# Attention and routed experts in one kernel: an attention pipeline one block deeper, and expert 0's rescaling moved between engines

## The chip, the cores and the metric

The kernel runs on one core of one Trainium2 chip. A core has a matrix engine (TensorE, in the profile PE, with its weight loads shown as PEld), VectorE (DVE), ScalarE (ACT), GpSimd (POOL) and SyncE (SP), each with its own queue of instructions that it works through in order, and 16 DMA engines that they share. The metric is device time in microseconds (us) for one execution. Matrix results land in PSUM, from where DVE or ACT copies them on; all other data lies in SBUF.

## What is computed

Eight batches of causal attention with a window of 128 and a slope per head (8 heads, 576 tokens, head size 64) give x, 4608 tokens of 512 values. Then a gate gives each token a weight for each of eight experts, balanced by eight rounds of row and column normalisation, and every expert is applied to every token:

```python
rel = pos[:, None] - pos[None, :]
mask = (rel >= 0) & (rel < 128)
scores = where(mask, scale * q @ k.T - slopes * abs(rel), -1e9)
x = softmax(scores) @ v                  # [4608, 512] after the heads are joined

P = exp(x @ w_gate - max)                # [4608, 8]
for _ in range(8):
    P /= P.sum(1, keepdims=True) + 1e-09
    P /= P.sum(0, keepdims=True) + 1e-09
    P *= N / E
for e in range(8):                       # D = 512, F = 1024
    out += P[:, e:e + 1] * (relu(x @ w1[e]) @ w2[e])
```

## The kernel before

The order of all instructions is written out by hand, so the place of a call in the Python text is its place in its engine's queue.

**Attention (lines 132 to 423).** The 576 tokens of a batch are five blocks of 128 (the last has 64); 40 blocks in all, loop index `i`, batch `b`, block `kb`. For a block, `scores(b, kb, half)` (line 209) multiplies keys and queries for four heads into the PSUM tile psS (one tile of two banks, used by both halves in turn), ACT takes the exponential (line 224) and DVE multiplies by the mask (line 230). `attend` (line 238), called through `finish(i - 1)` for the block before, multiplies by V into psN0 and psN1, one bank for each group of four heads, and DVE divides each group by its row sum (lines 268 and 269) into xsb. `put_x` (line 295), called through `finish2(i - 1)`, transposes xsb on PE into psXT and DVE copies it to xT, the array x of the experts. `gates` (line 279) multiplies xT by the gate's weights.

The queries and keys of the next batch are prepared meanwhile: `load_qk` (line 143, on POOL's queue, three buffers for four loads per batch), `turn` (line 169, two DVE copies, one for k and one for q, each into a buffer of its own), `tr_unit` (line 180, PE transposes; k is copied to KT by ACT, q to QZ by two DVE copies). Block kb of a batch does `tr_unit` for j = kb - 1, for k and for q.

Between these, PE is filled with work of expert 0: a group is 512 tokens, `l1(ft)` is one unit (four matmuls of 512 columns, relu on ACT), `l2(ms)` is two units (eight matmuls, copied to acc by DVE in line 322). `fill(most)` (line 333) takes units from the list while `credit` lasts; a block earns RATE = 2.75. Groups 0 to 5 are done this way, 96 units. psT, psXT, psG, psh and psy share the four buffers of tag pmm. `finish2` adds a group to the list once its tokens are in xT.

**Expert 0's rest and the balancing (lines 450 to 501).** DVE and POOL do the eight rounds on P_sb, while PE runs groups 6 to 8 of expert 0 (`e0_l1`, `e0_l2`, copies on ACT). The last round writes Pe_sb. Then PE transposes P (line 492), DVE copies it (line 497), SP stores it to PTd, and `load_p` (line 511) loads the factors of a step back, broadcast over partitions, as Pb.

**Experts 1 to 7 (lines 503 to 699).** 63 steps, expert `e`, group `g`. `make_xs` multiplies xT by Pb, two DVE operations per step. In a step PE alternates seven products of layer 2 of this step (`product`, eight matmuls of 256 columns each, by a scheme that needs seven products of quarters where eight would be plain; `make_s` and `make_t` prepare its sums) with eight pieces of layer 1 of the next step (`l1s`). The products go to four banks m0 to m3; `gather` (line 604, DVE) adds a bank to a quarter of acc. Before the first gather on a group, acc must hold expert 0's result times its factor, with the quarter (1, 1) subtracted from two others: `convert(g)` (line 609) does this on POOL, four multiplies (line 615) and two subtracts (line 618) per group, all nine groups being queued ahead of step 0. `quad(g, rh, ch)` names a quarter, two blocks of 256 columns.

Of the kernel before, what the change touches and what calls it, by code (L numbers as in the profile page):

```python
# [14 lines left out]
def kernel(  # L15
# [32 lines left out]
    RATE = 2.75  # L48
# [83 lines left out]
    with (  # L132
# [36 lines left out]
        def turn(b: int, half: int):  # L169
            for nm in ("k", "q"):  # L170
                tt = asb.tile(
                    [RP, RT, 4 * Dh], FP16, name=f"{nm}p_{b}_{half}", tag=f"{nm}p", bufs=1
                )
                nc.vector.tensor_copy(
                    out=tt.rearrange("p r (h d) -> p r h d", d=Dh),
                    in_=raw.pop((nm, b, half)).rearrange("p h (r d) -> p r h d", d=Dh),
                )
                turned[nm] = tt
# [30 lines left out]
        def scores(b: int, kb: int, half: int):  # L209
            k0 = kb * P  # L210
# [4 lines left out]
            for jj in range(2):  # L215
# [14 lines left out]
            nc.vector.tensor_tensor(  # L230
                out=pt[0:nk, :, 0:nq],
                in0=pt[0:nk, :, 0:nq],
                in1=maskT[0:nk, 4 * half : 4 * half + 4, 0:nq],
                op=ALU.mult,
            )
            return pt

        def attend(b: int, kb: int, pts, prev):
# [3 lines left out]
            xsb = asb.tile([P, H, Dh], FP16, name=f"xsb_{b}_{kb}", tag="xsb", bufs=2)  # L242
            for hg in range(2):
                psN = aps.tile([P, 4, Dh + 1], FP32, name=f"psN{hg}_{b}_{kb}", tag=f"psN{hg}")
# [14 lines left out]
                for i, (hh, lhsT, rhs) in enumerate(ops):  # L259
                    nc.tensor.matmul(  # L260
                        out=psN[0:nk, hh, :],
                        lhsT=lhsT,
                        rhs=rhs,
                        start=(i == 0),
                        stop=(i == len(ops) - 1),
                    )
                rden = asb.tile([P, 4], FP32, name=f"rden_{b}_{kb}_{hg}", tag="rden", bufs=2)
                nc.vector.reciprocal(out=rden[0:nk, :], in_=psN[0:nk, :, Dh])
                nc.vector.tensor_tensor(
                    out=xsb[0:nk, 4 * hg : 4 * hg + 4, :],  # L270
                    in0=psN[0:nk, :, 0:Dh],
                    in1=rden[0:nk, :].unsqueeze(2).to_broadcast([nk, 4, Dh]),
                    op=ALU.mult,
                )
# [39 lines left out]
        def add_group(g: int):  # L314
# [5 lines left out]
            def l2(ms):  # L320
                psy = l2_mm(0, g, ms, hT0[g], aps, "pmm", 4)
                nc.vector.tensor_copy(out=acc(4 * g + ms), in_=psy)  # L322
# [18 lines left out]
        with tc.manual_schedule():  # L341
# [20 lines left out]
            turn(0, 0)  # L362
# [17 lines left out]

            for i, (b, kb) in enumerate(blocks):
# [4 lines left out]
                a0 = scores(b, kb, 0)  # L386
                if i == 0:
                    turn(0, 1)
# [43 lines left out]
    with (  # L432
# [46 lines left out]
        def e0_l2(g):  # L479
            for ms in range(4):  # L480
                psy = l2_mm(0, g, ms, hT0[g], mps, f"m{ms}", 1)
                nc.scalar.copy(out=acc(4 * g + ms), in_=psy)
# [17 lines left out]
        )  # L500
        e0_l2(NG - 1)

# [106 lines left out]
        def convert(g):  # L609

            for ms in range(2):
                for rh in range(2):
                    p = Pe_sb[:, 0, 4 * g + 2 * rh + ms : 4 * g + 2 * rh + ms + 1]
# [116 lines left out]
```

## Time and profile before

| what | us |
|---|---|
| median of 3 runs | 1129.45 (1129.07 to 1130.6) |
| the profiled execution | 1128.04 |
| its span, first to last instruction | 1126.3 |
| start of block 6 of attention | 51.03 |
| first piece of group 6 of expert 0 | 238.62 |
| transposes of P | 276.08 |
| first product of expert 1 | 291.67 |

A row of the timeline reads: start, duration, engine, line, operation, what it writes and reads, shapes, count, and in brackets the idle time before it and what ended that. Matmuls are pipelined and a row's duration includes the time until the last result is out, so the price of one is read from start to start. L322 is line 322.

### The profile page before, as it was taken

How to read it: one execution, taken by the hardware profiler on the slowest of the kernel's cores; microseconds unless marked ns; L12 is line 12 of the kernel's file. 1: busy time of each engine (PE TensorE's matmuls, PEld its weight loads, DVE VectorE, ACT ScalarE, POOL GpSimd, SP SyncE). 2: the span in 40 equal slices, each digit the busy share in tenths (PEclk: the TensorE clock that was granted, in tenths of full speed). 3: DMA queues.
4: the chain of work that ended last, by engine and by line, in shares of the span. 5: the costliest groups of instructions: out<-in, count | busy, mean ns of one | idle time of the engine just before them, and what ended most of it. 6: DMA issues, size and time to landing. Idle time of an engine off the chain costs nothing.

```text
span 1126.3 us, 18273 instructions
## 1 busy us (share of the span) xinstructions
PE 1061.8 (94%) x7675; PEld 672.0 (60%) x7675; DVE 819.3 (73%) x1320; ACT 439.2 (39%) x737; POOL 166.2 (15%) x155
## 2 busy tenths in 40 slices
PE   3898899899699999999999999999999999999996
PEld 2454455444366666666666666666666666666664
DVE  5777777664498886777676877677777777788885
ACT  3455556534233333333333333333333333333331
POOL 5332222001499700000000000000000000000000
PEclk9999999989899999999999999999999999999999
DMA  9976758122301041003300230014000500003333
GB/s 156 107 73 67 69 62 79 32 40 51 77 20 29 20 75 39 19 20 65 57 19 20 57 57 29 20 26 88 19 20 28 94 20 19 20 10 94 98 97 97
DMA packets 78451, 58.86 MB, mean 52 GB/s; under 512 B 43648, under 2 KB 61472, under 8 KB 78368
## 3 DMA queue, kind: packets, MB, share of 16 engines
q0 software_dynamic: 63376, 30.96, 22.2%
q1 hardware_dynamic: 14992, 26.73, 7.7%
q8 instruction: 60, 0.98, 0.4%
q14 instruction: 23, 0.19, 0.1%
HBM read 79.02 MB, written 9.58 MB: 79 GB/s over the span
## 4 chain that ended last, share of the span: by engine, by line
PE 86%; DVE 6%; ACT 3%; DMA 2%; POOL 1%; issue 1%; DVEq 0%; POOLq 0%; SPq 0%
DMA qf_0_107<-in_q_dram 1%; POOL acc_lo L615 1%; DMA kf_0_82<-in_k_dram 1%; POOL vsb_77 L162 0%; DMA Pb_0_3693<-PTd 0%; DVE acc_hi L607 0%; PE psy_11_1903 L120 0%; POOL acc_lo L618 0%; DVE acc_lo L322 0%; DVE xs_0_3699 L524 0%; DVE xT L309 0%; DMA PTd<-PT_sb 0%; PE M_7_4_11391 L595 0%; PE M_7_5_11530 L595 0%; PE M_7_2_11113 L595 0%
## 5 line engine op out<-in xcount | busy, mean ns | idle before, releaser
L106 PEld LDWEIGHTS <-w1t_103 128*128 128x128 f16 x288 | 27.4, 101 | 32.5 <-issue 6.9
L615 POOL TENSOR_SCALAR acc_lo<-acc_lo,Pe_sb 128x512 f32<-128x512 f32 x24 | 42.1, 1768 | 12.3 <-issue 12.3
L537 PEld LDWEIGHTS <-w1t_2990 128*128 128x128 f16 x288 | 28.4, 98 | 23.9 <-issue 2.2
L537 PEld LDWEIGHTS <-w1t_4981 128*128 128x128 f16 x288 | 28.2, 98 | 20.5
L537 PEld LDWEIGHTS <-w1t_9661 128*128 128x128 f16 x288 | 28.2, 98 | 20.5
L537 PEld LDWEIGHTS <-w1t_6151 128*128 128x128 f16 x288 | 28.2, 98 | 20.5
L537 PEld LDWEIGHTS <-w1t_3689 128*128 128x128 f16 x288 | 28.2, 98 | 20.5
L537 PEld LDWEIGHTS <-w1t_8491 128*128 128x128 f16 x288 | 28.2, 98 | 20.5
L537 PEld LDWEIGHTS <-w1t_7321 128*128 128x128 f16 x288 | 28.2, 98 | 20.5
L615 POOL TENSOR_SCALAR acc_hi<-acc_hi,Pe_sb 128x512 f32<-128x512 f32 x12 | 21.7, 1820 | 0.0
L618 POOL TENSOR_TENSOR acc_lo<-acc_lo 128x512 f32<-128x512 f32 x12 | 17.9, 1514 | 0.5
L162 POOL DMA_DIRECT2D vsb_77<-in_v_dram x20 | 17.1, 877 | 0.3 <-PE psS_1_1_589 L216 0.3
L216 PEld LDWEIGHTS <-KT_73 128*128 128x128 f16 (+1 forms) x80 | 7.5, 111 | 16.1 <-issue 13.4
L162 POOL DMA_DIRECT2D vsb_78<-in_v_dram x20 | 16.9, 874 | 0.0
L95 POOL DMA_DIRECT2D w1t_9661<-in_moe_w_dram x1 | 0.8, 754 | 105.5 <-DVE T_9527 L573 105.5
L95 POOL DMA_DIRECT2D w1t_8491<-in_moe_w_dram x1 | 0.8, 752 | 105.0 <-PE psh_8_7_8351 L537 105.0
L95 POOL DMA_DIRECT2D w1t_7321<-in_moe_w_dram x1 | 0.8, 752 | 105.0 <-PE psh_8_7_7181 L537 105.0
L95 POOL DMA_DIRECT2D w1t_6151<-in_moe_w_dram x1 | 0.8, 752 | 105.0 <-PE psh_8_7_6011 L537 105.0
L285 PEld LDWEIGHTS <-xT 128*128 128x128 f16 x144 | 8.2, 99 | 8.3 <-DVE xT L309 1.5
L216 PEld LDWEIGHTS <-KT_74 128*128 128x128 f16 (+1 forms) x80 | 6.6, 101 | 9.0 <-issue 5.5
L595 PE MATMUL M_1_0_3819<-w2t_3358,hT_0_3759 128*128 128x256 f16 x16 | 2.9, 342 | 7.8 <-DVE acc_lo L607 7.8
L607 DVE TENSOR_TENSOR acc_lo<-acc_lo,M_1_0_3819 128x512 f32<-128x512 f32 x2 | 1.4, 680 | 11.9 <-POOL acc_lo L618 11.9
(3629 smaller groups left out, 3076.9 us busy)
## 6 DMA issues: line engine op xcount, KB each, us to landing
out_dram<-acc_lo SPq DMA_DIRECT2D x48, 128.0 KB
out_dram<-acc_hi SPq DMA_DIRECT2D x24, 128.0 KB
vsb_77<-in_v_dram POOLq DMA_DIRECT2D x16, 128.0 KB, 5.1
vsb_78<-in_v_dram POOLq DMA_DIRECT2D x16, 128.0 KB, 5.2
w1t_103<-in_moe_w_dram POOLq DMA_DIRECT2D x1, 1024.0 KB, 8.2
w2t_113<-in_moe_w_dram POOLq DMA_DIRECT2D x1, 1024.0 KB, 12.3
w1t_2990<-in_moe_w_dram POOLq DMA_DIRECT2D x1, 1024.0 KB, 10.5
w2t_3358<-in_moe_w_dram POOLq DMA_DIRECT2D x1, 1024.0 KB, 9.7
```

Of the source, the lines that this page charges most:

```text
L95: nc.gpsimd.dma_start(out=w1ts[e], in_=w1v)
L106: nc.tensor.matmul(out=psh, lhsT=w1t[:, dt, P * ft : P * ft + P], rhs=xT[:, dt, GT * g : GT * g + GT], start=(dt == 0), stop=(dt == NDT - 1),)
L162: nc.gpsimd.dma_start(out=vsb[0:nk, kb, :, 0:Dh], in_=v[b, :, k0 : k0 + nk, :].rearrange("h s d -> s h d"),)
L216: nc.tensor.matmul(out=ps[0:nk, jj, :, 0:nq], lhsT=KT[:, 2 * half + jj, k0 : k0 + nk], rhs=QZ[:, 2 * half + jj, :, k0 : k0 + nq],)
L285: nc.tensor.matmul(out=psG, lhsT=xT[:, dt, P * blk : P * blk + P], rhs=wg_sb[:, dt, :], start=(dt == 0), stop=(dt == NDT - 1),)
L537: nc.tensor.matmul(out=psh, lhsT=w1ts[e][:, dt, P * ft : P * ft + P], rhs=xss[i][:, dt, :], start=(dt == 0), stop=(dt == NDT - 1),)
L595: nc.tensor.matmul(out=ps[:, ms, :], lhsT=a[:, kt, P * ms : P * ms + P], rhs=b[:, kt, :], start=(first and ms == 0 and kt == 0), stop=(kt ...
L607: nc.vector.tensor_tensor(out=t, in0=t, in1=banks[bank], op=op)
L615: nc.gpsimd.tensor_scalar(out=y, in0=y, scalar1=p, scalar2=None, op0=ALU.mult)
L618: nc.gpsimd.tensor_tensor(out=t, in0=t, in1=quad(g, 1, 1), op=ALU.subtract)
```

## The change

- Attention: `put_x` and the gates of a block come two blocks after its scores, where it was one, and stand between the two halves of scores, as does the first transpose unit; xsb gets a third buffer. The mask is a function of its own: mask0 comes after the first fill and the copy of k, mask1 after `attend`. `turn` takes k or q; k is copied ahead of mask0, q at the end of the block (in block 0 both at the end).
- Division: psN0 and psN1 become one tile of two banks, with one reciprocal and one multiply for all eight heads.
- The copy of expert 0's layer 2 in attention goes from DVE to ACT. RATE is 2.85.
- P's transposes come after two of the four layer 2 pieces of group 7, with the DVE copy and the store.
- `convert` goes. `rescale` does its multiplies on ACT, `rebase` its subtracts on DVE: group 0 before layer 2 of group 8, groups 1 to 8 one in each of the first eight steps. The calls of load_w1(2) and load_w2(2) stand in another place of the text, after the same instructions of their queue.

```diff
-    RATE = 2.75
+    RATE = 2.85
...
-        def turn(b: int, half: int):
-            for nm in ("k", "q"):
+        def turn(b: int, half: int, nm: str):
...
             nc.scalar.activation(
...
-            nc.vector.tensor_tensor(
-                out=pt[0:nk, :, 0:nq],
...
-            return pt
+            def mask():
+                nc.vector.tensor_tensor(
+                    out=pt[0:nk, :, 0:nq],
...
+            return pt, mask
...
-            xsb = asb.tile([P, H, Dh], FP16, name=f"xsb_{b}_{kb}", tag="xsb", bufs=2)
+            xsb = asb.tile([P, H, Dh], FP16, name=f"xsb_{b}_{kb}", tag="xsb", bufs=3)
+            psN = aps.tile([P, 2, GT], FP32, name=f"psN_{b}_{kb}", tag="psN")
+            psV = psN[:, :, 0 : 4 * Dh + 4].rearrange("p g (h d) -> p g h d", d=Dh + 1)
             for hg in range(2):
-                psN = aps.tile([P, 4, Dh + 1], FP32, name=f"psN{hg}_{b}_{kb}", tag=f"psN{hg}")
...
-                        out=psN[0:nk, hh, :],
+                        out=psV[0:nk, hg, hh, :],
...
-                rden = asb.tile([P, 4], FP32, name=f"rden_{b}_{kb}_{hg}", tag="rden", bufs=2)
-                nc.vector.reciprocal(out=rden[0:nk, :], in_=psN[0:nk, :, Dh])
-                nc.vector.tensor_tensor(
-                    out=xsb[0:nk, 4 * hg : 4 * hg + 4, :],
...
+            rden = asb.tile([P, 2, 4], FP32, name=f"rden_{b}_{kb}", tag="rden", bufs=2)
+            nc.vector.reciprocal(out=rden[0:nk], in_=psV[0:nk, :, :, Dh])
+            nc.vector.tensor_tensor(
+                out=xsb[0:nk].rearrange("p (g h) d -> p g h d", g=2),
+                in0=psV[0:nk, :, :, 0:Dh],
+                in1=rden[0:nk].unsqueeze(3).to_broadcast([nk, 2, 4, Dh]),
+                op=ALU.mult,
+            )
...
                 psy = l2_mm(0, g, ms, hT0[g], aps, "pmm", 4)
-                nc.vector.tensor_copy(out=acc(4 * g + ms), in_=psy)
+                nc.scalar.copy(out=acc(4 * g + ms), in_=psy)
...
-                a0 = scores(b, kb, 0)
+                pt0, mask0 = scores(b, kb, 0)
                 if i == 0:
-                    turn(0, 1)
+                    turn(0, 1, "k")
+                    turn(0, 1, "q")
                     for j in range(2, 4):
                         tr_unit(0, "k", j)
                         tr_unit(0, "q", j)
-                fill(1)
-                a1 = scores(b, kb, 1)
-                pts[i] = (a0, a1)
+                if i > 2:
+                    gates(done)
                 if i > 1:
-                    gates(done)
+                    done = finish2(i - 2, xsbs.pop(i - 2))
                 if units:
                     tr_unit(*units[0])
+                fill(1)
+                turning = kb in (0, 2) and b + 1 < B
+                if turning and i > 0:
+                    turn(b + 1, kb // 2, "k")
+                mask0()
+                pt1, mask1 = scores(b, kb, 1)
+                pts[i] = (pt0, pt1)
                 if i > 0:
-                    xsb = finish(i - 1)
+                    xsbs[i - 1] = finish(i - 1)
+                mask1()
                 fill(2)
                 if units:
                     tr_unit(*units[1])
-                if i > 0:
-                    done = finish2(i - 1, xsb)
                 fill(1)
-                if kb in (0, 2) and b + 1 < B:
-                    turn(b + 1, kb // 2)
+                if turning:
+                    if i == 0:
+                        turn(1, 0, "k")
+                    turn(b + 1, kb // 2, "q")
...
             credit = 1e9
-            fill(1)
+            xsbs[i] = finish(i)
             gates(done)
-            xsb = finish(i)
+            done = finish2(i - 1, xsbs[i - 1])
             fill(2)
-            done = finish2(i, xsb)
+            gates(done)
+            done = finish2(i, xsbs[i])
             fill(1 << 20)
             gates(done)
...
-        def e0_l2(g):
-            for ms in range(4):
+        def e0_l2(g, mss=range(4)):
+            for ms in mss:
...
+        def rescale(g):
+
+            for blk in range(4 * g, 4 * g + 4):
+                nc.scalar.mul(acc(blk), acc(blk), Pe_sb[:, 0, blk : blk + 1])
+
+        def rebase(g):
+
+            for rh in range(2):
+                t = quad(g, rh, 1 - rh)
+                nc.vector.tensor_tensor(out=t, in0=t, in1=quad(g, 1, 1), op=ALU.subtract)
+
         g0 = NHI // 4
         e0_l1(g0)
         for g in range(g0 + 1, NG):
             e0_l1(g)
-            e0_l2(g - 1)
+            if g < NG - 1:
+                e0_l2(g - 1)
+        e0_l2(NG - 2, range(2))
         psP = mps.tile([P, 3, P], FP32, name="psP", tag="psP")
...
+        e0_l2(NG - 2, range(2, 4))
+        rescale(0)
+        rebase(0)
         e0_l2(NG - 1)
+        load_w1(2)
+        load_w2(2, per, "w2a")
...
-        load_w1(2)
-        load_w2(2, per, "w2a")
         for i in range(3):
             load_p(i)
         make_xs(0)
         make_xs(1)
-        for g in range(NG):
-            convert(g)
...
             gather(i, 3, 1, 1, ALU.add)
+            if i + 1 < NG:
+                rescale(i + 1)
             if i + 2 < NS:
                 make_xs(i + 2)
+            if i + 1 < NG:
+                rebase(i + 1)
```

More of the change, by code (lines that the diff above doesn't have):

```diff
@@ L167 @@
         turned: dict = {}
-        def turn(b: int, half: int):
-            for nm in ("k", "q"):
[L171 to L178, printed above, removed]
+        def turn(b: int, half: int, nm: str):
+            tt = asb.tile(
+                [RP, RT, 4 * Dh], FP16, name=f"{nm}p_{b}_{half}", tag=f"{nm}p", bufs=1
+            )
+            nc.vector.tensor_copy(
+                out=tt.rearrange("p r (h d) -> p r h d", d=Dh),
+                in_=raw.pop((nm, b, half)).rearrange("p h (r d) -> p r h d", d=Dh),
+            )
+            turned[nm] = tt
         def tr_unit(b: int, nm: str, j: int):
@@ L361 @@
             groups = 0
-            turn(0, 0)
+            turn(0, 0, "k")
+            turn(0, 0, "q")
             for j in range(2):
@@ L379, in finish2 @@
                 return done
+            xsbs: dict = {}
+            done = 0
             for i, (b, kb) in enumerate(blocks):
@@ L607, in gather @@
             nc.vector.tensor_tensor(out=t, in0=t, in1=banks[bank], op=op)
[L609 to L613, printed above, removed]
-                    y = acc(4 * g + 2 * rh + ms)
-                    nc.gpsimd.tensor_scalar(out=y, in0=y, scalar1=p, scalar2=None, op0=ALU.mult)
-            for rh in range(2):
-                t = quad(g, rh, 1 - rh)
-                nc.gpsimd.tensor_tensor(out=t, in0=t, in1=quad(g, 1, 1), op=ALU.subtract)
         def settle(g, rh, ch):
```

13 lines of the change are left out of this document (5 added, 8 removed).

## The prediction

> **What bounds the kernel now.** I read the busy lines first, then the windows by stage (columns: length, then busy us and count of PE, PEld, DVE, ACT, POOL, then granted clock, DMA share, GB/s).
>
> ```profile
> PE 1061.8 (94%) x7675; PEld 672.0 (60%) x7675; DVE 819.3 (73%) x1320; ACT 439.2 (39%) x737; POOL 166.2 (15%) x155
> 28.00:45.00 17.00, 12.59 (x135) 8.49 (x136) 12.31 (x35) 6.33 (x12) 5.71 (x8) 1.00 1.48 152
> 51.03:238.62 187.59, 165.42 (x1669) 92.32 (x1668) 138.46 (x340) 98.34 (x169) 42.15 (x53) 0.97 0.59 62
> 238.62:283.50 44.88, 44.86 (x199) 19.85 (x200) 22.46 (x50) 20.95 (x36) 4.15 (x9) 0.93 0.30 58
> 283.50:311.00 27.50, 18.61 (x103) 10.49 (x103) 13.45 (x18) 8.35 (x14) 14.78 (x11) 0.88 0.32 58
> 600.00:700.00 100.00, 100.00 (x678) 66.25 (x677) 73.64 (x104) 36.84 (x62) 1.64 (x2) 1.00 0.20 40
> ```
>
> PE is the engine that sets the time. From 311 us on it has no gap at full clock, so nothing there can be gained without fewer matmuls, and the change removes none. What can move lies before: attention (to 238.62, where group 6 of expert 0 begins) and the passage to expert 1 (283 to 311). The list of waits says who holds PE there (total, times, longest), and the timeline shows the passage:
>
> ```profile
> PE M_1_0_3819 L595 <- DVE acc_lo L607: 7.8, 1, 7.8
> ...
> PE psXT_1_3165 L300 <- DVE xsb_1_3140 L269: 2.0, 2, 1.8
> ```
>
> Rows of this second kind, one for nearly every block, are the main thing in attention: put_x transposes xsb in the same block in which DVE divides it, and DVE reaches that division only after both masks.
>
> **Part 1: the block pipeline.** A block whose waits are small gives the prices on PE, start to start:
>
> ```profile
> 56.41 0.59 PE L216 MATMUL psS_2_0_651<-QZ_76,KT_74 128*128 128x512 f16 x2
> 56.84 1.03 PE L106 MATMUL psh_0_5_657<-xT,w1t_103 128*128 128x512 f16 x4
> 58.11 0.59 PE L216 MATMUL psS_2_1_663<-QZ_76,KT_74 128*128 128x512 f16 x2 [0.25 <-ACT pt_2_0_654 L224]
> 58.54 0.24 PE L285 MATMUL psG_669<-wg_sb,xT 128*128 128x8 f16 x4
> 58.65 0.42 PE L185 MATMUL psT_k_1_675<-ident,kp_0_568 72*128 72x72 f16 x8
> 58.90 0.29 PE L260 MATMUL psN_1_1_686<-vsb_78,pt_0_0_509 128*128 128x65 f16 x4
> ...
> 59.41 1.02 PE L106 MATMUL psh_0_6_710<-xT,w1t_103 128*128 128x512 f16 x4
> 60.28 1.03 PE L106 MATMUL psh_0_7_716<-xT,w1t_103 128*128 128x512 f16 x4
> 61.14 0.42 PE L185 MATMUL psT_q_1_722<-ident,qp_0_570 72*128 72x72 f16 x8
> 61.40 0.53 PE L300 MATMUL psXT_1_733<-ident,xsb_1_685 128*128 128x128 f16 x4
> 61.77 0.49 PE L216 MATMUL psS_3_0_743<-QZ_76,KT_74 128*128 128x384 f16 x2
> ```
>
> A half of scores is 0.43 (56.41 to 56.84), a unit of filler 0.87 (59.41 to 60.28), a gate 0.11, a set of q or k transposes 0.25, attention times V 0.51 (58.90 to 59.41), put_x 0.37. Without filler a full block is 0.86 + 0.11 + 0.50 + 0.51 + 0.37 = 2.35; blocks 3 and 4 of a batch have narrower scores, block 0 no transposes, so I take 2.1 as the mean (1.9 to 2.35). From 51.03 (block 6) to 238.62 PE has 34 blocks x 2.1 = 71, less 2 for the last batch's absent transposes, plus 94 units x 0.87 = 82 (six groups of 16, two units done), plus 1 for the last block's remainder: 152 us of work in 187.6. **So 36 us are stalls**, and DVE (138 of 188 busy) and ACT (98) are not full.
>
> After the change, in a block at t=0: scores 0.43, gates 0.11, put_x of the block two back 0.37, a transpose 0.25, a unit 0.87, then the second half of scores at 2.0. In the row at 58.11 that half started 1.70 after the first, released by the exponentials; 2.0 is later, so this wait (0.25 where it shows) goes. put_x's division was done a block earlier, so the psXT waits go. DVE loses two small operations per block and the copies of layer 2; ACT gains the copies:
>
> ```profile
> 160.69 0.69 DVE L322 COPY acc_lo<-psy_12_2221 128x512 f32<-128x512 f32 x1
> ...
> 271.10 0.59 ACT L482 COPY acc_hi<-psy_28_3603 128x512 f32<-128x512 f32 x1 [1.13 <-PE psy_28_3603 L120]
> ...
> 224.09 0.17 DVE L268 RECIPROCAL rden_1_0_3150<-psN_7_1_3141 128x4 f32<-128x4 f32 x1
> 224.30 0.42 DVE L269 TENSOR_TENSOR xsb_1_3140<-psN_7_1_3141,rden_1_0_3150 128x256 f16<-128x256 f32 x1
> 224.65 0.17 DVE L268 RECIPROCAL rden_1_1_3162<-psN_7_1_3153 128x4 f32<-128x4 f32 x1
> 224.78 0.28 PE L300 MATMUL psXT_1_3165<-ident,xsb_1_3140 128*128 128x128 f16 x2 [1.78 <-DVE xsb_1_3140 L269]
> ```
>
> 24 x 0.69 = 17 us leave DVE and 24 x 0.59 = 14 come to ACT (98 + 14 = 112 in what would be about 170: covered on average). The pair of divisions is 2 x 0.55 (224.09 to 224.65); as one, a recip of 0.2 and a multiply of 512 elements between 0.42 and 0.84, taken as 0.69 from L322: 0.2 us less per block. Regrouping makes the multiply wait for both head groups; behind it on DVE stand mask1 and the q copies, whose reader is a block away. turn for k now stands ahead of mask0 and splits from q: its data were loaded a batch earlier, its release lets POOL's fourth q/k load and the V loads behind it start a little sooner, and DVE delays mask0 by one copy, whose reader is again a block away.
>
> What is late next? Three things. (a) Where the first fill takes a two-unit piece and the second is empty (about 8 of the 34 blocks by the credit rule), the next scores come 0.43 + 0.51 + 0.25 = 1.2 after the last ones, and 1.7 to 1.9 are needed: 8 x 0.6 = 5. (b) The first fill needs the pmm buffer of the previous block's last q transpose, which DVE frees with two copies of the size of L269's 0.42 behind mask1, some 1.3 after that block's end; PE asks at 1.1: 0.2 in 27 blocks, 5. (c) ACT runs in order with a copy, a k copy, a gate and two exponentials per block: 0.15 x 34 = 5. The end keeps its own chain (mask, division, transpose, copy, gate): 4. That is 19 left of 36, **17 gained** (bounds: 5 if the new waits double, 27 if only the end's and (a) remain). RATE 2.85 for 2.75 only offsets that filler starts a block later: 96 units are consumed either way.
>
> The start: before 45 us PE idles 4.4 of 17 in the window quoted, on the same two kinds of waits, and the first batch's transposes wait behind mask0:
>
> ```profile
> 16.26 0.66 PE L185 MATMUL psT_k_2_176<-ident,kp_1_172 72*128 72x72 f16 x8 [2.45 <-DVE kp_1_172 L174]
> ...
> 31.69 1.01 PE L216 MATMUL psS_2_1_290<-QZ_75,KT_73 128*128 128x512 f16 x2 [1.11 <-ACT pt_2_0_287 L224]
> ```
>
> With turn(0, 1) ahead of mask0 some 1.5 return there, and of the 4.4 most. A new wait: turn(1, 0, "q") and turn(1, 1, "q") hold DVE until their loads land, and the second half of block 1's scores now stands behind a transpose that waits too. I take **5** (0 to 7).
>
> **The clock.** Three short stretches of attention ran at half clock (the first and the last are shown, with what stood before the first), though no wait there is over 1.8:
>
> ```profile
> 72.00:76.00 4.00, 3.62 (x32) 2.02 (x30) 2.58 (x5) 2.12 (x3) 0.00 (x0) 1.00 0.00 0
> ...
> 76.30:79.70 3.40, 2.44 (x9) 0.98 (x10) 2.55 (x8) 0.93 (x1) 0.71 (x2) 0.65 0.00 0
> ...
> 202.60:206.00 3.40, 2.66 (x10) 0.86 (x10) 2.42 (x7) 0.38 (x1) 0.00 (x0) 0.65 0.01 1
> ```
>
> Each costs half of 3.4, together 5, and is in the 36. I count them as returned, as denser work should not trip them. The Trainium skill (TensorE: Matmul & The Clock Gate, Part 1) says that the clock falls after at least one idle window of about 3.4 us. This trace does not agree: the stretch before the first fall was 3.62 of 4.00 busy. By that rule the falls would have another cause than these waits and would stay, which is a rival below.
>
> **Part 2: the passage to expert 1.**
>
> ```profile
> 276.08 0.49 PE L492 MATMUL psP<-identf,Pe_sb 128*96 128x128 f32 x3
> ...
> 282.79 2.36 DVE L524 TENSOR_TENSOR xs_0_3699<-xT,Pb_0_3693 128x1024 f16<-128x1024 f16 x2 [5.62 <-DMA Pb_0_3693<-PTd]
> ...
> 284.06 0.59 PE L537 MATMUL psh_0_0_3760<-xs_0_3699,w1t_2990 128*128 128x512 f16 x2 [0.58 <-DVE xs_0_3699 L524]
> ...
> 285.20 0.59 PE L537 MATMUL psh_0_0_3760<-xs_0_3699,w1t_2990 128*128 128x512 f16 x2 [0.54 <-DVE xs_0_3699 L524]
> ...
> 306.57 1.86 PE L595 MATMUL M_1_0_3819<-w2t_3358,hT_0_3759 128*128 128x256 f16 x8 [7.79 <-DVE acc_lo L607]
> ...
> 308.23 1.61 PE L537 MATMUL psh_1_4_3899<-xs_1_3702,w1t_2990 128*128 128x512 f16 x4
> ...
> 309.68 1.04 PE L595 MATMUL M_1_0_3856<-T_3808,hT_0_3759 128*128 128x256 f16 x8
> ```
>
> and the groups of POOL's convert on the page (busy, mean ns of one, idle before):
>
> ```profile
> L615 POOL TENSOR_SCALAR acc_lo<-acc_lo,Pe_sb 128x512 f32<-128x512 f32 x24 | 42.1, 1768 | 12.3 <-issue 12.3
> ...
> L618 POOL TENSOR_TENSOR acc_lo<-acc_lo 128x512 f32<-128x512 f32 x12 | 17.9, 1514 | 0.5
> ```
>
> PE stops 7.79 at 306.57 because the first gather waits for POOL's convert; two pieces then run at half clock: 306.57 to 308.23 is 1.66 for 0.87 and on to 309.68 is 1.45 for 0.87, 1.4 lost. ACT rescales group 0 during expert 0, so all **9.2** go. P's transposes move ahead of two pieces of layer 2 (2 x 1.73), with their DVE copy, the PTd store and, behind it on SP, the Pb loads. From 276.08 the factors took 6.7 to land; PE now has 3.5 + 6.9 = 10.4 of work over that. New on the way: rescale(0) on ACT follows the copies of group 7 (4.6 after the transposes), 4 x 0.6, then rebase(0) on DVE, 2 x 0.69, ahead of make_xs(0): 8.3, then two halves of 1.18, done at 10.7; the second half is asked for at 11.1. The 0.58 + 0.54 go: **1.1**, with 0.4 us to spare. The weight loads for expert 2 keep their place in POOL's queue.
>
> In expert 1, each of eight steps (13.0 us, fifteen sets of 0.87) gets 4 ACT multiplies and 2 DVE subtracts. ACT is free at 7.8 into the step; the subtracts wait for it, and behind them on DVE stands gather(0, 0, 0), which must end before the next step's first product overwrites bank 0 at 13.0. Free time: 13.0 - 7.8 - 0.7 = 4.5 for 4a + 2d. The trace has no such multiply on ACT: a lies between 0.59 (L482) and 1.77 (L615), d between 0.69 (L322, a DVE operation of that size) and 1.51 (L618). I take the low ends, the rows of the same engines: 3.7, hidden. At the high ends it is 10.1, 5.6 over, 45 us in eight steps. The Trainium skill (ScalarE: Activation LUTs, What ACT_TABLE_LOAD costs) gives 186 ns plus 0.833 ns an element and 93 ns for a per-partition operand; by it, an estimate, a is 0.71 and the sum does not change, though its rules for authors send such multiplies to VectorE.
>
> **The sum.** 17 + 5 + 9.2 + 1.1 = 32.3 us off the profiled execution of 1128.04 (span 1126.3): 1095.7. The median of the runs shown is 1.4 higher: **1097**. Bounds of the terms alone: 5 + 0 + 8 (the stop alone) + 0 = 13 gives 1116, 27 + 7 + 9.2 + 1.1 = 44 gives 1085.
>
> **Rivals.**
>
> - ACT becomes what attention waits for: the layer 2 copies sit in order ahead of exponentials. For: a full block has two exponentials of 1.02 (row below) and four copies of 0.59, 4.4 of the 4.8 that PE needs with its share of filler. Against: 112 of 170 on average. New waits 28 instead of 19, start 3: 1108. Chance 0.22.
> ```profile
> 214.91 1.02 ACT L224 ACTIVATE pt_1_0_3062<-psS_1_0_3059 128x1024 f16<-128x1024 f32 x1 [0.20 <-PE psS_1_0_3059 L216]
> ```
>
> - The clock falls stay, as the page has it: 5 less gained, 1102. Chance 0.10.
> - Attention moves its waits and gains nothing; only the passage pays: 1119. Chance 0.06. That the pipeline does not do what it says is this case.
> - The new waits stay at 9: 1087. Chance 0.06.
> - Slower: the rescaling chain ACT to DVE costs in the steps of expert 1 what it cost on POOL. -32 + 45 gives 1142. It decides from 4a + 2d above 4.5 + 32/8 = 8.5 per step. Against it stand the rows of L482 and L322. Chance 0.03.
>
> The forecast, 1089 to 1104, has 0.53. With the neighbours the range that holds 8 in 10 is **1084 to 1112**; it leaves out the third and the last case and the edges of others. A measurement of this kernel can tell about 0.2% (2.3 us) from no change. Faster 0.96, same 0.01, slower 0.03.
>
> **What would show it.** No psXT wait on xsb and no half clock between 50 and 200 us; group 6 of expert 0 starting near 217 instead of 238.6; no wait of M_1_0 at L607 and no xs wait after the P transposes; steps of expert 1 still 13.0; ACT multiplies near 0.6. It is wrong if PE waits on the pmm buffers or exponentials for over 0.5 us a block, or if DVE's gather comes after 13.0.

## The result: 1094.4 us, and the profile after

| | before | after |
|---|---|---|
| median, us | 1129.29 (4 runs) | 1094.4 (1092.01 to 1095.43, 4 runs) |
| the profiled execution | 1128.04 | 1093.95 |
| its span | 1126.3 | 1092.2 |

The ratio after to before is 0.9686, with an interval of [0.9668, 0.9704]. The kernel is 3.1% faster. Forecast were 1097 us and a range of 1084 to 1112.

First the busy line of the page of after, and its windows by stage (columns as before: length, busy us and count of PE, PEld, DVE, ACT, POOL, then granted clock, DMA share, GB/s):

```profile
PE 1051.2 (96%) x7675; PEld 671.6 (61%) x7675; DVE 795.8 (73%) x1234; ACT 471.1 (43%) x797; POOL 77.2 (7%) x101
```
```profile
37.80:51.40 13.60, 11.93 (x104) 7.28 (x104) 9.88 (x22) 6.00 (x12) 5.35 (x7) 0.54 1.46 141
51.40:211.80 160.40, 153.93 (x1633) 89.96 (x1630) 113.52 (x238) 108.35 (x190) 39.80 (x48) 1.00 0.66 67
211.80:218.60 6.80, 5.50 (x36) 2.53 (x35) 4.46 (x11) 1.56 (x5) 0.39 (x1) 0.58 1.02 148
280.70:293.70 13.00, 13.00 (x90) 8.59 (x89) 10.46 (x15) 7.05 (x12) 0.00 (x0) 1.00 0.08 20
600.00:700.00 100.00, 100.00 (x676) 65.91 (x674) 74.39 (x106) 36.53 (x62) 1.64 (x2) 1.00 0.21 43
```

The number of matmuls is the same, 7675. From block 6 to group 6 of expert 0 PE was 88% busy before (165.42 of 187.59); now it is 96% from 51.4 to 211.8 (153.93 of 160.40), and its clock is full there but for the first 1.1 us. Two half-clock stretches stand on either side, 38.8 to 52.5 and 212.9 to 219.7. The second was there before as well (a granted clock of 0.58 from 236.7 to 243.5); what the first means is said under "The start" below. A step of expert 1 is 13.0 us, without a gap, with the rescaling inside it. From there on nothing has changed.

The timeline of after has the landmarks. Its columns are start, duration, engine, line, operation, output and inputs:

```profile
46.32 1.03 PE L216 MATMUL psS_1_0_532<-QZ_76,KT_74 128*128 128x512 f16 x2
...
214.56 1.87 PE L106 MATMUL psh_6_0_3257<-xT,w1t_103 128*128 128x512 f16 x4
...
248.17 0.49 PE L520 MATMUL psP<-identf,Pe_sb 128*96 128x128 f32 x3
...
259.65 0.59 PE L570 MATMUL psh_0_0_3552<-xs_0_3545,w1t_2842 128*128 128x512 f16 x2 [0.20 <-DVE xs_0_3545 L557]
...
266.13 1.04 PE L628 MATMUL M_1_0_3611<-w2t_3198,hT_0_3551 128*128 128x256 f16 x8
...
273.07 1.04 PE L628 MATMUL M_1_0_3611<-w2t_3198,hT_0_3551 128*128 128x256 f16 x8
```

Read against the landmarks of before, they say where the 34.1 us of span went:

- Block 6 starts at 46.32 instead of 51.03, but two units of filler (2 x 0.87) have moved behind it. The start gave 4.7 - 1.7 = **3.0**.
- From block 6 to group 6 of expert 0: 168.2 us instead of 187.6, with those two units more in it: 19.4 + 1.7 = **21.1**.
- From group 6 to P's transposes 33.6 instead of 37.5, of which 3.5 are the two pieces that moved behind them: 0.4.
- From P's transposes to the first product of expert 1: 17.96, less those 3.5, is 14.5. Before it was 291.67 - 276.08 = 15.6: **1.1**.
- From there to the row at 273.07, the product that waited 7.79 us at 306.57: 6.94 instead of 14.90, **8.0**, and 1.4 for the half clock behind it.
- Step 8 of expert 1 lost 0.6: M_1_8_4733 waits for a sum of `make_s` on DVE.

Together 34.3, against the 34.1 that the spans show.

### The profile page after: what moved, and what is told of

Read it like the earlier page. It is cut to its first block, busy times and chain, and to the rows that moved or that the text cites. A ratio compares the mean times of both kernels' runs of the same rounds, so it can differ in the third digit from the quotient of the medians.

```text
span 1092.2 us, 18188 instructions
## 1 busy us (share of the span) xinstructions
PE 1051.2 (96%) x7675; PEld 671.6 (61%) x7675; DVE 795.8 (73%) x1234; ACT 471.1 (43%) x797; POOL 77.2 (7%) x101
## 4 chain that ended last, share of the span: by engine, by line
PE 91%; DMA 3%; DVE 2%; ACT 1%; POOL 1%; issue 1%; DVEq 0%; ACTq 0%; POOLq 0%
DMA kf_0_404<-in_k_dram 1%; DMA kf_0_105<-in_k_dram 1%; DMA kf_0_82<-in_k_dram 1%; DVE acc_hi L640 0%; POOL vsb_77 L162 0%; POOL vsb_78 L162 0%; DMA Pb_0_3539<-PTd 0%; ACT acc_hi L502 0%; DVE xs_0_3545 L557 0%; PE M_1_8_4733 L628 0%; PE psy_17_2624 L120 0%; PE psy_11_1828 L120 0%; PE psy_18_2704 L120 0%; PE psy_15_2303 L120 0%; PE M_7_7_11644 L628 0%
## 5 line engine op out<-in xcount | busy, mean ns | idle before, releaser
L162 POOL DMA_DIRECT2D vsb_77<-in_v_dram x20 | 18.6, 943 | 0.3 <-PE psG_537 L289 0.3
L162 POOL DMA_DIRECT2D vsb_78<-in_v_dram x20 | 18.2, 926 | 0.0
L508 DVE TENSOR_TENSOR acc_lo<-acc_lo 128x512 f32<-128x512 f32 x12 | 7.8, 688 | 10.9 <-ACT acc_lo L502 10.9
L502 ACT ACTIVATE acc_lo<-acc_lo,Pe_sb 128x512 f32<-128x512 f32 x24 | 15.3, 710 | 0.0
L644 DVE TENSOR_TENSOR acc_lo<-acc_lo 128x512 f32<-128x512 f32 x12 | 8.3, 692 | 0.4
```

Source lines behind the costliest of these rows:

```text
L162: nc.gpsimd.dma_start(out=vsb[0:nk, kb, :, 0:Dh], in_=v[b, :, k0 : k0 + nk, :].rearrange("h s d -> s h d"),)
L502: nc.scalar.mul(acc(blk), acc(blk), Pe_sb[:, 0, blk : blk + 1])
L508: nc.vector.tensor_tensor(out=t, in0=t, in1=quad(g, 1, 1), op=ALU.subtract)
L644: nc.vector.tensor_tensor(out=t, in0=t, in1=quad(g, 1, 1), op=ALU.add)
```

## The experiments

Each time is a median, each ratio that kernel to the kernel before (1129.91 to 1130.81 us in those sessions), with its interval.

**Do the two parts add?** In the first kernel only attention is changed, with the passage (convert on POOL, P's transposes late) as before; in the second only the passage is changed.

> The attention of the changed kernel with the passage to expert 1 of the kernel before (convert on POOL, P's transposes after all of group 7). Theory: the two parts add. Attention took 24 us of the 34 (group 6 of expert 0 began at 214.6 instead of 238.6), so 1129.3 - 24 = 1105 (1102 to 1108), the stop of 7.8 before M_1_0 is there again, and the first piece of group 6 begins at 214.6 as in the changed kernel. Rival: attention only moves its gain into the passage, because the balancing rounds start earlier beside the same PE work; then a part of the 24 is lost again ahead of P's transposes and the time is above 1108.

> The attention of the kernel before with the passage of the changed kernel (rescale on ACT, rebase on DVE, P's transposes two pieces earlier). Theory: 10 us of the 34 are here (7.8 of stop, 1.4 of half clock, 1.4 around the transposes, less 0.6 for a late sum in step 8), 1129.3 - 10 = 1119.5 (1117.5 to 1121); attention keeps its waits of psXT on xsb and its three stretches at half clock. Rival: the passage gains more where attention is slower, or nothing without it: 1115 or 1128.

Measured: attention alone **1103.52** (0.9762 [0.9726, 0.9799]), the passage alone **1119.91** (0.991 [0.988, 0.994]), each within the range of its theory. That is 26.4 and 10.0 us off, 36.4 together, where the whole gives about 35: they add. The list of waits of the first shows that the old stop stays where it was when only attention is changed (waiter and line, releaser and line: us in total, times, longest):

```profile
PE M L610 <- DVE acc_lo L622: 7.5, 1, 7.5
```

**Is it the depth that serves attention?** Three kernels, each from the kernel after. First, put_x again one block after its scores, at the old place in the block:

```diff
-                if i > 2:
-                    gates(done)
                 if i > 1:
-                    done = finish2(i - 2, xsbs.pop(i - 2))
+                    gates(done)
...
                     tr_unit(*units[1])
+                if i > 0:
+                    done = finish2(i - 1, xsbs.pop(i - 1))
```

> The changed kernel with put_x one block after its scores again, at its old place behind the second transpose, the division still ahead of mask1. Theory A (of the prediction): the depth removes the waits of psXT; without it about 10 of the 24 us return, 1104 (1100 to 1110), with psXT waits on xsb of 0.5 or more in most blocks. Theory B: what removes them is that the division stands ahead of mask1 with a fill behind it, the extra block adds little but cover between the two halves of scores: 1094 to 1098, psXT waits under 0.3, and instead the second half of scores waits 0.1 to 0.3 for the exponential.

Measured: **1125.45** (0.9965 [0.9946, 0.9985]); both expectations missed. Its waits between 28 and 245 us name the reason:

```profile
PE psG L289 <- DVE xT L313: 25.6, 29, 1.3
PE psXT L304 <- DVE xsb L273: 9.4, 12, 1.0
```

The gates now stand between the halves of scores, right behind the put_x of the block before, and wait for its copy into xT. That is a fault of my edit, not a price of the depth, so the second kernel puts the gates behind the second half of scores, where they were before the change.

> As the one-deep run before, but with the gates where the kernel before had them, behind the second half of scores. That run held 26 us of waits of psG on the copy into xT, 11 of psXT on xsb: the first kind came from the gates' place in front. Theory B (the order carries the gain, the depth covers the rest): the psG waits go, the 11 us of psXT stay, some of it beside other slack: 1094.4 + 6 to 11, 1100 to 1106. Theory A (depth is what counts): the wait moves again, 1110 or more. Theory C: nothing is left of the depth's worth, 1094 to 1097.

Measured: **1096.54** (0.9705 [0.969, 0.9719]), 2.1 us above after, with intervals that overlap: theory C. The depth alone is not what makes this kernel fast. Yet waits of psXT are left (51 to 238 us):

```profile
PE psXT L304 <- DVE xsb L273: 8.7, 10, 1.0
```

The third keeps two blocks of depth and puts mask1 back ahead of `attend`, and so ahead of the division on DVE:

```diff
                 pts[i] = (pt0, pt1)
+                mask1()
                 if i > 0:
                     xsbs[i - 1] = finish(i - 1)
-                mask1()
```

> The changed kernel, two deep, with mask1 ahead of the division on DVE again. With a block more of depth the division has until the next block's put_x, some 2.5 us more than it takes, so nothing waits: 1094 to 1097, no psXT waits over 0.3. Rival: the division must come early even at this depth, since PE asks for psN's banks and xsb a block later while DVE stands on the exponential: 1100 to 1108 with waits on xsb.

Measured: **1103.92** (0.977 [0.9755, 0.9785]), 9.5 us lost although the division has a block more, the rival's range; its waits of psXT in the same stretch:

```profile
PE psXT L304 <- DVE xsb L273: 10.0, 13, 1.0
```

So the place of mask1 matters with the depth in place. The two rows are alike and the times are not, so the total of this one wait is no price. All waits of PE on the lists from 51 to 238 us, which is past attention's end, are 10.1 us in the second kernel, 15.9 in the third and 7.5 in after. Two more kernels ask what it does without the depth. One takes before's attention (with after's passage, 1119.91 above) and moves nothing but mask1:

```diff
-                a1 = scores(b, kb, 1)
+                a1, mask1 = scores(b, kb, 1)
...
                 if i > 0:
                     xsb = finish(i - 1)
+                mask1()
```

> The attention of the kernel before with one thing changed, mask1 behind the division instead of ahead of it, and the passage of the changed kernel (so 1119.9 is the time without it). The one-deep run with the gates later lost only 2 us to the changed kernel, and the two-deep run with mask1 first lost 9. Theory: the place of mask1 is the largest single part: the 20.9 us of psXT waits fall below 8 and the stretches at half clock go, 1119.9 - 12 to 16 = 1104 to 1108. Rival: it is spread, the transposes between the two halves, one division for two and the copies on ACT each carry a share, and mask1 alone gives under 6: 1114 or more.

Measured: **1100.57** (0.9742 [0.9727, 0.9758]), 19.3 us for one instruction per block moved in DVE's order, more than either range allowed. The other is the kernel after with both undone, put_x one block deep (gates late) and mask1 ahead:

> The kernel after with both cures undone: put_x one block after its scores, at the block's end, the gates behind the second half of scores, and mask1 ahead of attend and the division. Known: both in place 1094.4, put_x one block earlier alone 1096.5, mask1 ahead alone 1103.9. Theory (the two are two ways to the same slack between division and put_x, so that either alone covers most of the stall): without both, psXT waits in nearly every block with longest ones near 2 us, as in the attention of before, and 1109 to 1120. Rival (the place of mask1 costs the same 9.5 us wherever put_x stands, so the two add): 2.1 + 9.5 on 1094.4, 1104 to 1108.

Measured: **1121.63** (0.9917 [0.9897, 0.9937]), 1.6 above the upper end of the theory's range and far from the rival's. The four corners, the rest of the new attention being the same in all but for the gates' place:

| | mask1 ahead of the division | mask1 behind it |
|---|---|---|
| put_x one block after its scores, gates late | 1121.63 | 1096.54 |
| put_x two blocks after | 1103.92 | 1094.4 (after) |

The depth is worth 17.7 us where mask1 stands ahead and 2.1 where it stands behind; moving mask1 is worth 25.1 at one block and 9.5 at two. These times also hold the start and the end, whose half clock differs from kernel to kernel. From the first scores of block 8 to those of block 38 (57.77 to 202.67 in after), less 0.87 for each unit of filler between them, the traces give 91.5 us for the kernel with neither, 76.9 with the depth alone, 70.5 with mask1 behind alone and 69.2 for after. There the depth is worth 14.6 and 1.3, moving mask1 21.0 and 7.7. **They are two ways to the same slack, and either one brings most of it.** Without both, all of attention's gain is gone: 1121.63 against the 1119.91 of before's attention.

The waits between 51 and 238 us, first of the kernel with neither, then of the one with only mask1 moved, say the same:

```profile
PE psXT L304 <- DVE xsb L273: 23.6, 21, 2.1
PE psS L216 <- ACT pt L224: 0.5, 2, 0.2
```
```profile
PE psXT L303 <- DVE xsb L272: 6.5, 20, 0.9
PE psS L216 <- ACT pt L224: 2.5, 10, 0.2
```

Why one instruction weighs so much is read from the block with the 1.61 us wait in the timeline of before:

```profile
163.02 0.59 PE L216 MATMUL psS_1_1_2262<-QZ_76,KT_74 128*128 128x512 f16 x2
163.65 1.02 ACT L224 ACTIVATE pt_1_1_2265<-psS_1_1_2262 128x1024 f16<-128x1024 f32 x1 [1.13 <-PE psS_1_1_2262 L216]
163.71 0.30 PE L260 MATMUL psN_5_0_2279<-vsb_78,pt_0_0_2175 128*128 128x65 f16 x4
...
164.71 0.69 DVE L230 TENSOR_TENSOR pt_1_1_2265<-pt_1_1_2265,maskT 128x1024 f16<-128x1024 f16 x1 [0.73 <-ACT pt_1_1_2265 L224]
165.32 0.17 DVE L268 RECIPROCAL rden_0_0_2284<-psN_5_0_2279 128x4 f32<-128x4 f32 x1
...
166.01 0.29 PE L300 MATMUL psXT_0_2306<-ident,xsb_0_2278 128*128 128x128 f16 x2 [1.61 <-DVE xsb_0_2278 L269]
```

psN_5_0 was done at 164.01. DVE could have divided then, and was idle: it stood 0.73 us at mask1, which waits for an exponential of 1.02, and then worked 0.6 on the mask. The division began at 165.32, 1.3 late, and PE waited 1.61. The same block after the change:

```profile
148.52 0.59 PE L216 MATMUL psS_1_1_2172<-QZ_76,KT_74 128*128 128x512 f16 x2
...
149.08 0.29 PE L264 MATMUL psN_0_2178<-vsb_78,pt_0_1_2087 128*128 128x65 f16 x4
...
149.40 0.21 DVE L272 RECIPROCAL rden_0_2187<-psN_0_2178 128x8 f32<-128x8 f32 x1 [1.28 <-PE psN_0_2178 L264]
149.65 0.69 DVE L273 TENSOR_TENSOR xsb_0_2177<-psN_0_2178,rden_0_2187 128x512 f16<-128x512 f32 x1
150.26 0.69 DVE L232 TENSOR_TENSOR pt_1_1_2175<-pt_1_1_2175,maskT 128x1024 f16<-128x1024 f16 x1
```

DVE now waits for psN and divides within 0.1 us of its end; xsb is complete at 150.34, 1.8 after the second half of scores began, before the next block's scores are out. The mask comes at 150.26, when its exponential has just ended, and no longer waits. PE still stands 0.65 us here, but for the exponential itself (psS_2_0_2202, started at 150.28), not for the division.

**The copies of layer 2.** From the kernel after, they go back to DVE in attention:

```diff
-                nc.scalar.copy(out=acc(4 * g + ms), in_=psy)
+                nc.vector.tensor_copy(out=acc(4 * g + ms), in_=psy)
```

> The changed kernel with the layer 2 copies of attention on DVE again. Theory: DVE was not what PE waits for once the pipeline is deeper (119 busy of 168), and ACT has as little room in full blocks as DVE: within 2 us of the changed kernel, 1092.5 to 1096.5. Rival 1: moving them was a real part of the gain; back on DVE they delay the masks and the division, 1098 to 1104. Rival 2: ACT is what PE waits for now (waits of psS on the exponential and of the pmm buffers on P_sb), and taking 14 us off it gains: 1089 to 1092.

Measured: **1097.03** (0.9702 [0.9672, 0.9732]). A loss of 2.6 with overlapping intervals, between the ranges of the theory and of rival 1. The traces are sharper than the medians: from the first scores of block 8 to those of block 38, with the same 87 units of filler, this kernel takes 147.90 us, after 144.90, and two other kernels with after's attention (attention alone, and the next but one below) 144.89 each. So in these traces the copies' engine is worth 3.0 us.

**How far is ACT's rescaling from the bound?** In groups 1 to 8 the multiplies of `rescale` are issued twice, so expert 0's part is multiplied by its factor twice there:

```diff
                 nc.scalar.mul(acc(blk), acc(blk), Pe_sb[:, 0, blk : blk + 1])
+                if g > 0:
+                    nc.scalar.mul(acc(blk), acc(blk), Pe_sb[:, 0, blk : blk + 1])
```

> The changed kernel with each multiply of rescale for groups 1 to 8 issued twice, so that expert 0's part is multiplied by its factor twice there. In the changed kernel the four take 2.55 us in a step and gather(0, 0, 0) ends some 0.9 us before the next step's first product needs its bank. Theory of the prediction (the chain ACT, rebase, gather has a free time and costs one to one beyond it): 2.55 - 0.9 = 1.65 in eight steps, 13 us: 1107 (1103 to 1112), with waits of the first product of steps 1 to 8 on L640. Rival 1: DVE catches up before PE asks, the free time is larger: 1094 to 1098. Rival 2: ACT's delay of relu holds PE through the three psh buffers as well: 1114 or more.

Measured: **1115.49** (0.9867 [0.9844, 0.989]), the range of rival 2. The waits from 270 to 430 us:

```profile
PE psh L572 <- ACT hT L579: 11.4, 8, 1.4
PE M L630 <- DVE acc_lo L642: 2.5, 6, 0.4
```

What binds first is not the bank that the gather frees, as my sum had it, but ACT's relu: the relus of layer 1 stand behind the multiplies in its queue, and PE finds no free buffer for the next piece. Half clock came on top (last section).

**The start.** The k load for block 1 meets the 1 MB load of w1 and lands late. Here it is issued ahead of it:

```diff
-            load_w1(0)
             load_qk(1)
+            load_w1(0)
```

> The changed kernel with the q and k loads of batch 1 issued ahead of expert 0's w1. In the changed kernel PE stood 6.8 us in block 1 on the turn of k, whose load was issued at 15.8 behind w1 and landed at 26.2. Theory: that load sets the start, so 3 to 7 us go: 1088 to 1091, with block 2 beginning near 24 instead of 29.9. Rival: the next loads (the fourth of batch 1, w2, V of batch 1, then batch 2) come later in the same queue and give it back by block 6: 1093 to 1096.

Measured: **1094.88** (0.9686 [0.9669, 0.9702]), no change, as the rival had it. The wait moves: psXT now waits 11.5 us once, for a division that stands on DVE behind a copy of k, and that copy stood 11.05 us until its load had landed (47.28):

```profile
PE psXT L304 <- DVE xsb L273: 13.2, 4, 11.5
```

**The end of attention.** Six units of filler are kept for the last two blocks (RATE 2.65) and laid between their transposes and divisions:

```diff
-    RATE = 2.85
+    RATE = 2.65
...
             credit = 1e9
+            fill(1)
             xsbs[i] = finish(i)
...
-            fill(1 << 20)
+            fill(1)
             gates(done)
+            fill(1 << 20)
```

> The changed kernel with RATE 2.65 instead of 2.85, so that 6 of the 96 units of expert 0 are left for the end of attention, and placed there: two before the last product with V, two behind the put_x before the last, two behind the last. In the changed kernel the end held 1.0 (psN on the division), 0.9 and 0.4 (psG on xT) of waits and 6.8 us at half clock, 3.4 lost. Theory: the units fill the waits and keep the clock up: 2.3 to 5.7 less, 1089 to 1092. Rival: the thinner fill of the blocks before opens as many waits (0.2 units less in each of 34 blocks), or the clock falls all the same: 1093 to 1096.

Measured: **1087.9** (1086.88 to 1089.82; 0.9628 [0.9612, 0.9645]). It beats both kernels, and after by 6.5 us, more than the theory's 2.3 to 5.7. Its windows from 51.1 us on:

```profile
51.10:210.00 158.90, 154.73 (x1649) 90.22 (x1647) 114.79 (x242) 107.63 (x191) 39.71 (x48) 1.00 0.70 74
210.00:224.00 14.00, 14.00 (x70) 6.38 (x69) 10.20 (x24) 9.63 (x17) 1.59 (x4) 1.00 0.01 2
```

Group 6 begins at 210.24, 4.3 earlier than in after, and at full clock; in after its first four pieces took 5.99 us (214.56 to 220.55) instead of 4 x 0.87. 4.3 + 2.5 = 6.8 is the gain, against 6.9 between the two spans.

**The place of P's transposes.** They come after all four pieces of group 7 again, the rest as after:

```diff
-        e0_l2(NG - 2, range(2))
+        e0_l2(NG - 2)
...
-        e0_l2(NG - 2, range(2, 4))
```

> The changed kernel with P's transposes behind all four pieces of group 7 again. In the changed kernel xs_0 began 9.1 us after the transposes and PE then waited 0.2; the store to PTd took 4.6 instead of 2.0. Theory: the factors come 3.46 later against the same PE work, so PE stands some 3 us before the first piece of expert 1: 1097 to 1098.5; that is more than the 1.1 which the prediction gave the move, since rebase and the slower store would stand in the way without it. Rival: the store was slow only because it met the w1 load, and is fast 3.5 us later: 1094.5 to 1095.5.

Measured: **1094.16** (0.9678 [0.9661, 0.9695]): no difference, and not the theory's 3 us. The store is fast again, as the rival had it (2.05 us, last section). PE's waits on xs return, 0.48 and 0.54, but the end of the kernel does not come later by an amount that can be measured.

## Why the prediction was right, and where it was not

The time was right, 1097 against 1094.4, and so was the sum by parts; the step that explains the largest term was only half of the cause.

- **The block pipeline (17; measured 21.1). The step "put_x's division was done a block earlier, so the psXT waits go" names one of two sufficient causes, and the one that does less here.** mask1 leaving the division's way on DVE is a second one, and in the kernel as it stands the larger: taking it back costs 9.5 us, taking the depth back 2.1. I had read in the trace that "DVE reaches that division only after both masks", and in the change mask1 behind the division appeared to me only as something that had become later. I took the slack from the depth alone. It does not suffice: with the depth and mask1 ahead, psXT still waits 10.0 us in 13 places, and all waits together are 15.9 us where after has 7.5. Nor was there such a wait "for nearly every block" before: the list from block 6 to the end has them for 20 of 34 blocks.
- The size of what is left was too high. 168.2 us less 153.5 of work by the prediction's own prices (34 blocks, 96 units) leaves about 15 us of stalls, where I had 19. Of these, 7.5 are on the list of waits and 3.9 are lost to half clock (up to 52.5 and from 212.9); the rest has no row of its own. The new waits came where I put them, but smaller. These rows of the waits of after show one of each kind, the exponentials in turn (7 rows, 2.9 us), the gate's exponential on ACT, which frees a buffer of tag pmm (5 rows, 2.0), the q copies (1 row), and the end's own chain (3 rows, 2.3):

```profile
PE psN_4_3132 L264 <- DVE xsb_3_3109 L273: 1.0, 1, 1.0
PE psG_3164 L289 <- DVE xT L313: 0.9, 1, 0.9
PE psS_2_0_2202 L216 <- ACT pt_1_1_2175 L224: 0.7, 1, 0.7
...
PE psy_15_2303 L120 <- ACT P_sb L296: 0.4, 1, 0.4
...
PE psh_1_1_1029 L106 <- DVE QZ_76 L203: 0.3, 1, 0.3
```

  The term (b), a pmm buffer behind the q copies in 27 blocks, was 5 and is 0.3: in its place PE waits now and then for ACT's gate. The rival "ACT becomes what attention waits for" (1108) fell with 2.9 + 2.0 us of such waits.
- **The clock.** That the three stretches inside attention would go was right: none is left from 51.4 to 211.8. The rival by which they stay (1102) fell. The one at attention's end stayed, since its waits stayed (211.8 to 218.6); the end-fill kernel shows that it goes when they are filled. One reading behind this step was wrong: "3.62 of 4.00 busy" is not what stood right before the first fall. The clock fell at 77.30, and in the 3.41 us ahead of that PE was busy 1.96 (rows in the last section). A thin stretch ahead of the fall is a better ground for "denser work should not trip them" than the row that I gave.
- **The start (5; measured 3.0).** The wait that I named and then gave no price has come, and it is as long as those that went: PE's waits from 14 us to block 6 add to about 12 us before and 11 after, where most of it is the second of these rows:

```profile
19.18 1.01 PE L216 MATMUL psS_1_0_228<-QZ_75,KT_73 128*128 128x512 f16 x2 [1.11 <-ACT pt_0_1_221 L224]
26.99 0.66 PE L184 MATMUL psT_k_0_233<-ident,kp_0_224 72*128 72x72 f16 x8 [6.80 <-DVE kp_0_224 L173]
```

  The second half of block 1's scores stands behind a transpose that waits 6.80 us for the k load. Then the granted clock is half from 38.8 to 52.5: the half of scores at 46.32 takes 1.03, where it takes 0.59 in the rows of before at 56.41 and 58.11. But before ran its start no faster. Its half of scores at 31.69 took 1.01, though the granted clock of that window reads 1.00; the next to take 0.59 is at 47.33. In after it is the same until 34 us (1.01 at 32.04). So that column does not show the rate of the first 46 and 34 us, and the stretch from 38.8 on is a loss against before only from 47 to 52.5. Since issuing the load earlier changed nothing, the load's place alone doesn't mend the start.
- **The passage (9.2; measured 8.0 + 1.4).** As predicted, and alone it gives 10.0. The chain that replaces POOL's stays hidden. These rows of the timeline show the last multiplies of a step, the subtracts behind them, the gather that had to be in time, and the product that it lets go:

```profile
300.42 1.93 ACT L502 ACTIVATE acc_lo<-acc_lo,Pe_sb 128x512 f32<-128x512 f32 x3
...
302.38 1.29 DVE L508 TENSOR_TENSOR acc_lo<-acc_lo 128x512 f32<-128x512 f32 x2 [0.98 <-ACT acc_lo L502]
...
303.60 0.68 DVE L640 TENSOR_TENSOR acc_lo<-acc_lo,M_1_2_3881 128x512 f32<-128x512 f32 x1
...
305.19 1.04 PE L628 MATMUL M_1_3_4016<-w2t_3198,hT_3_3890 128*128 128x256 f16 x8
```

  The gather ends at 304.28, 0.9 before it is needed. The multiply is longer than I took it: the group's row from 270 to 400 us has

```profile
L502 ACT ACTIVATE acc_lo<-acc_lo,Pe_sb 128x512 f32<-128x512 f32 x20 | 12.7, 710 | 0.0
L508 DVE TENSOR_TENSOR acc_lo<-acc_lo 128x512 f32<-128x512 f32 x10 | 6.5, 688 | 4.9 <-ACT acc_lo L502 4.9
```

  0.710 instead of 0.59, the subtract 0.688 as taken. The estimate from the Trainium skill (ScalarE: Activation LUTs, What ACT_TABLE_LOAD costs), 0.71, is what the trace shows. Free time of 4.5 for 4a + 2d was the right kind of sum with a wrong tenant: doubled multiplies cost 21 us, and first through the relu that stands behind them, not through the bank.
- **P's transposes (1.1; 1.1 in the trace, nothing in the median).** The wait on xs fell from 0.58 + 0.54 to 0.20, but without the move the time is the same. This term can't be told from zero.

## What to carry to other kernels

Where an engine runs in order, look at what stands ahead of the operation that the bottleneck waits for: an operation there that itself waits (here a mask for its exponential) delays everything behind it, and exchanging the two can be worth as much as a deeper pipeline. Before a gain is credited to one of several edits made together, take each back alone and both together, since two edits can fill the same slack, and taking back only one can then make it look nearly worthless. When a pipeline has become dense, its end is the next place to look: six units of filler kept for the last two blocks gave 6.5 us.

## What the runs showed of the hardware that was not expected

- **Half clock without a long stop.** In the kernel with doubled multiplies the granted clock fell three times for 3.4 us, though no wait of the list above was over 1.4 us. From 325 us to the first fall PE was 88% busy (12.70 of 14.50 up to 339.5), but that mean hides what stood right before it. Here are the 3.41 us on either side of the first fall:

```profile
337.21:340.62 3.41, 1.57 (x8) 0.53 (x7) 1.95 (x4) 3.24 (x7) 0.00 (x0) 1.00 0.03 9
340.62:344.04 3.42, 3.42 (x13) 1.82 (x13) 3.38 (x6) 0.21 (x1) 0.00 (x0) 0.50 0.00 0
```

  The other two, at 357.69 and 374.76, follow 1.57 of 3.41 as well. The same around the first of the three stretches of before:

```profile
73.89:77.30 3.41, 1.96 (x26) 1.25 (x23) 2.54 (x7) 1.09 (x2) 0.00 (x0) 1.00 0.00 0
77.30:80.71 3.41, 3.23 (x10) 1.22 (x11) 2.31 (x5) 1.25 (x2) 1.72 (x3) 0.50 0.12 8
```

  The other two of before follow 1.63 (135.33 to 138.74) and 1.81 (200.18 to 203.59). The Trainium skill (TensorE: Matmul & The Clock Gate, Part 1) has the clock fall after at least one idle window of about 3.4 us. These rows do not agree: PE was about half busy in those 3.41 us, not idle. Nor is half busy enough for a fall: from 162.63 to 166.04 in before PE was busy 1.80 of 3.41 and the clock stayed full. What else decides was not settled. A wait of 1 to 2 us that goes with such a fall costs more than its length, by half of the 3.4 us behind it.
- **A small store beside a large load.** The store of P's transposes, 96 rows, let the next loads on its queue begin 2.06 us after its issue before the change (277.19 to 279.25), 2.05 with the transposes late (249.59 to 251.64), and 4.61 in after:

```profile
245.18 0.77 POOL L95 DMA_DIRECT2D w1t_3535<-in_moe_w_dram  x1 [4.43 <-PE psh_8_7_3437 L106]
...
249.28 0.32 SPq L526 DMA_DIRECT2D PTd<-PT_sb  x1
...
253.89 0.33 SPq L547 DMA_DIRECT2D Pb_0_3539<-PTd  x1
```

  In after the load of w1 was issued 4.1 us ahead of the store, with the transposes late 7.6 ahead (242.03), before the change 7.6 ahead too (269.64). The packets in the traces say more. The load's last packet ends at 277.59 before the change, at 249.84 with the transposes late and at 253.04 in after. The store's first packet starts 0.83 us after its issue in the first two (278.02 and 250.42), when the load is over, and 3.15 us after it in after (252.43), when the load is nearly over. So the store stood while the load's packets moved; that the load is the cause was not tried alone.
